# Squares of the weights queued on ScalarE behind the fourth hh eviction of their group

## The chip, the cores and the metric

The kernel runs on one core of one Trainium2 chip. The metric is the device time of one execution in microseconds, median of several. Five engines work side by side, each through its own instruction queue in order: TensorE (PE: matmuls; PEld: its weight loads), VectorE (DVE), ScalarE (ACT), GpSimd (POOL) and SyncE (SP, which here only issues DMAs). They wait for each other through semaphores.

## The reference

Three stages follow each other: a linear attention with a root-mean-square norm, then a layer of 8 experts in which each token uses its two best experts, then a second one in which each token with a positive skip score uses its best expert. All 4608 tokens have 512 numbers.

```
kv = einsum('bhsd,bhse->bhde', k, v); out = einsum('bhsd,bhde->bhse', q, kv)   # 8 x 8 x 576 x 64
x = out / rms(out) * g_norm                                                     # as 4608 rows of 512
top2 = two best of x @ w_gate + log1p(exp(x @ w_noise)) * noise                 # first expert layer
out[mask] += top2_w * (max(x[mask] @ w1[e], 0) @ w2[e])                         # w1: 512 x 1024, w2: 1024 x 512
do_compute = out @ w_skip > 0; e_idx = argmax(out @ w_gate2)                    # second expert layer
result = out + do_compute * prob * (max(out @ w21[e], 0) @ w22[e])
```

## The kernel before

Precision is made of pairs of 16-bit numbers: each matrix and each activation is held as a high half (`hi`, `hh`, `wa` or `wb` first half) and a low half (`lo`, `hl`, second half), and each product is three matmuls. Before a weight matrix can be split into halves it has to be scaled by a power of two, and the scale comes from the sum of its squares. That work is in `split_matrix` (L157 to L183):

- the load of 2 MB into a `stage` buffer (two buffers, so a third load waits until the splits of the first are done),
- four squares on ACT, L166, each over 128 x 1024, with the row sums in `wacc`,
- the sum of the four on DVE (L169, `wsum`), a matmul with ones on PE that adds over the partitions (L172),
- six small operations on DVE that make the scale `wscl` (L128 to L133, L175 to L178),
- four splits: the high half on ACT (L182), the low half on DVE (L183).

It is a generator: each `yield` hands back control, and the main loop calls `next` at set points.

The first expert layer runs in 38 groups of 256 token slots, five groups to an expert (two of the first expert's were done earlier). The fifth group of an expert has 224 slots. One group (`moe1_group`) is: layer 1, four pieces of 24 matmuls (L219) into a PSUM tile `a` (three buffers), each piece followed by `layer1_out`: ACT writes `hh` (L227), then DVE writes `hl` (L228). Then layer 2 for the two halves g0 and g1 of the group, 24 matmuls each (L255) into a PSUM tile `b` (two buffers); its first 16 matmuls read `hh` piece by piece, four matmuls to a piece, the last 8 read `hl`. ACT evicts each half as `ysb` (L1014), DVE adds the earlier expert's rows (L1018, `x`), ACT and DVE make the 16-bit halves of the result (L870, L873, L874), a DMA transposes them (L889), and one group later PE computes routing logits from them (L894, L896), DVE turns them into a choice (L899 to L934, with `rm` at L930), and PE ranks the choices (L937 to L939) between layer 2 of one group and layer 1 of the next.

`MATS` says in which group which matrix is handled: F is a matrix of the first expert layer's next expert, P one of the second layer's (`presplit`, written back to DRAM), a dot none. Per expert the pattern is F P F . P or close to it. A matrix is loaded in its group n, squared at the points 4 to 7 of group n (which lie in layer 2), and scaled and split at the points 0 to 4 of group n+1: L172 stands after the first piece of layer 1, the splits after it.

The order on PE is written out by hand (`manual_schedule`). From group `BEGIN` (3) to group `CUT + 2` (35) the order on the other engines is set by a scheduler, which takes the instructions by priority and by its own idea of when each can start; `layer1_out` and `ysb` are raised by `URGENT`. In this stretch the squares stand on ACT wherever the scheduler found ACT free.

In the groups' names below, "wa group" means the group that splits a `wa` matrix, and so on: with the pattern F P F . P the five groups of an expert are a wa group, a presplit group, a wb group, a group of 224 slots that mostly splits nothing, and a presplit group.

Of the kernel before, what the change touches and what calls it, by code (L numbers as in the profile page):

```python
# [12 lines left out]
AF = mybir.ActivationFunctionType  # L13
# [5 lines left out]
N, D, E, F = 4608, 512, 8, 1024  # L19
# [60 lines left out]
def moe_kernel(ctx: ExitStack, tc: tile.TileContext, q, k, v, g_norm, w_gate, w_noise, noise,  # L80
               w1, w2, w2_skip, w2_gate, w21, w22, out, dbg=None):
    nc = tc.nc
    V, A, G, PE, SP = nc.vector, nc.scalar, nc.gpsimd, nc.tensor, nc.sync
# [3 lines left out]
    wpools = [ctx.enter_context(tc.tile_pool(name="wpool0", bufs=1))]  # L87
    turn = {}
    stg = [None]

    def wtile(shape, dt, name, pool=None):

        turn[name] = turn.get(name, -1) + 1
        return wpools[turn[name] % len(wpools) if pool is None else pool].tile(shape, dt, name=name)
# [29 lines left out]
    def pow2_scale(ss_ps, kk, name):  # L124

        n = ss_ps.shape[-1]
        t = tiny.tile([P, n], I32, name=name + "t")
        V.tensor_scalar(t, ss_ps.bitcast(I32), 24, None, op0=ALU.logical_shift_right)  # L128
        u = tiny.tile([P, 2, n], I32, name=name + "u")
        V.tensor_scalar(u[:, 0], t, -1.0, float(kk), op0=ALU.mult, op1=ALU.add)  # L130
        V.tensor_scalar(u[:, 1], t, 1.0, float(254 - kk), op0=ALU.mult, op1=ALU.add)
        s = tiny.tile([P, 2, n], I32, name=name + "s")
        V.tensor_scalar(s, u, 23, None, op0=ALU.logical_shift_left)  # L133
        f = s.bitcast(F32)
        return f[:, 0], f[:, 1]
# [21 lines left out]
    def split_matrix(load, hi, lo, scale, kk, sc, inv):  # L157

        st = stg[0].tile([P, 4096], F32, name="stage")
        load(st)  # L160
        acc = tiny.tile([P, 4], F32, name="wacc")
        junk = tiny.tile([P, F], BF16, name="wjunk", bufs=1)
        kw = {} if scale is None else {"scale": scale}
        yield
        for c in range(4):
            A.activation(junk, st[:, F * c:F * c + F], AF.Square, accum_out=acc[:, c:c + 1], **kw)  # L166
            if c == 3:
                sums = tiny.tile([P, 1], F32, name="wsum")
                V.tensor_reduce(sums, acc, axis=AX.X, op=ALU.add)  # L169
            yield  # L170
        ps = pSm[0].tile([P, 1], F32, name="small")
        PE.matmul(ps, ones32, sums, start=True, stop=True)  # L172
        a0, i0 = pow2_scale(ps, kk, "wsc")
        if scale is None:
            V.tensor_copy(sc, a0)  # L175
        else:
            V.tensor_mul(sc, a0, scale)
        V.tensor_copy(inv, i0)  # L178
        for c in range(4):
            yield  # L180
            d = slice(F * c, F * c + F)
            A.activation(hi[:, d], st[:, d], AF.Copy, scale=sc)  # L182
            V.scalar_tensor_tensor(lo[:, d], st[:, d], sc, hi[:, d], op0=ALU.mult, op1=ALU.subtract)  # L183

    def split_half(e, wa, wb, half, hi, lo, sc, scale):
        if half == 0:
            yield from split_matrix(
                lambda st: SP.dma_start(st.rearrange("p (c f) -> p c f", f=F), wa[e].rearrange("(c p) f -> p c f", p=P)),
                hi, lo, scale, 199, sc[:, 0:1], sc[:, 1:2])
        else:  # L190
            yield from split_matrix(
                lambda st: SP.dma_start(st.rearrange("p (c d) -> p c d", d=D), wb[e].rearrange("(c p) d -> p c d", p=P)),
                hi, lo, None, 204, sc[:, 2:3], sc[:, 3:4])
# [29 lines left out]
    def layer1_out(ps, nt, hh, hl, fp):  # L223

        nf = 512 // nt
        fsl = slice(fp * nf, fp * nf + nf)
        A.activation(hh[:, fsl, 0:nt], ps, AF.Relu)  # L227
        V.scalar_tensor_tensor(hl[:, fsl, 0:nt], ps, 0.0, hh[:, fsl, 0:nt], op0=ALU.max, op1=ALU.subtract)  # L228

    def layer1_piece(W, xT, nt, hh, hl, fp):  # L230
        ps = layer1_matmuls(W, xT, nt, fp)
        with tc.high_priority(offset=URGENT):
            layer1_out(ps, nt, hh, hl, fp)
# [741 lines left out]
    def gather1(e, i0):  # L975

        t0 = e * T1 + i0
        xg = p1.tile([P, 2, XW], F32, name="xg", bufs=3)
        xT = p1.tile([P, 8, 2 * P], F16, name="xT", bufs=3)
        for g in range(2):  # L980
            G.indirect_dma_start(out=xg[:, g], out_offset=None, in_=xrows,  # L981
                                 in_offset=bass.IndirectOffsetOnAxis(ap=idx1[:, t0 + g:t0 + g + 1], axis=0))
            SP.dma_start_transpose(out=xT[:, :, g * P:g * P + P], in_=xg[:, g, 0:512].bitcast(F16))
        return xg, xT
# [64 lines left out]
    def dyn_weights(wi, pool, W, half):  # L1049
        t = wtile([P, WB], F16, "wb", pool) if half else wtile([P, WA], F16, "wa", pool)  # L1050
        G.indirect_dma_start(out=t, out_offset=None, in_=wsd[half],
                             in_offset=bass.IndirectOffsetOnAxis(ap=wi, axis=0))
        W.extend(views(t, half))
# [136 lines left out]
    def matrix(m):  # L1190
        if m is None:
            return None
        kind, e, half = m
        if half == 0:
            gens[kind] = first_weights(e, w1, w2, gcol, 0.5, Ws[e]) if kind == "first" else presplit(e)
        return gens[kind][half]
# [11 lines left out]
    for n, (e, i0) in enumerate(groups):  # L1208
        if n == BEGIN:
            begin.close()  # L1210
        if n + 1 < len(groups) and n <= BEGIN:
            xs[n + 1] = gather1(*groups[n + 1])
        if n + 2 < len(groups) and n >= BEGIN:
            xs[n + 2] = gather1(*groups[n + 2])
        if n == CUT + 2:
            order.enter_context(tc.manual_schedule(engines=engines))
        old, cur = cur, matrix(mats[n])
        if cur:
            next(cur)

        def point(p, old=old, cur=cur):
            if old and p <= 4:
                next(old, None)
                if p == 4:
                    next(old, None)
            if cur and p >= 4:
                next(cur)

        def step(k, prev=fin, last=last):
            g = last if k == 0 else prev  # L1230
            if g is not None:
                next(g, None)
            if k == 0 and n == CUT + 2:
                pick_early()
            for i in range(2):
                for what in AHEAD[i].get((n, k), ""):
                    if what == "g":
                        Ra.append(Rows(ahead[i]))
                        for _ in range(2):
                            Ra[i].gather(osc[2 * (CUT + 1 - NF0):])  # L1240
                    elif what == "s":
                        Ra[i].split()
                    else:
                        dyn_weights(ewi[:, i:i + 1], 2 * i, Wa[i], "ab".index(what))

        step(-1)
        if n == CUT + 2:
            splits.close()
            wpools.append(only1.enter_context(tc.tile_pool(name="wpool2", bufs=1)))
            p3 = only1.enter_context(tc.tile_pool(name="p3", bufs=2))  # L1250
            p4 = xrow_pool.enter_context(tc.tile_pool(name="p4", bufs=1))
            for i in range(4):
                xo.append(p4.tile([P, 1, D], F32, name=f"x2r{i}"))
                G.memset(xo[i], 0.0)
        last = fin
        fin = moe1_group(e, i0, Ws[e], *xs.pop(n), step, point)
# [18 lines left out]
    nr, nt = len(RTILES), 4 + sum(RTILES)  # L1275
# [157 lines left out]
    with flag(0):  # L1433
# [5 lines left out]
        st, cur = 1, 0  # L1439
        while st < nf:  # L1440
            V.tensor_add(inc[:, 1 - cur, st:nf], inc[:, cur, st:nf], inc[:, cur, 0:nf - st])
            V.tensor_copy(inc[:, 1 - cur, 0:st], inc[:, cur, 0:st])
            cur, st = 1 - cur, st * 2
# [134 lines left out]
```

## Time and profile before

| what | value |
|---|---|
| median of 3 runs (lowest, highest) | 1336.52 us (1332.54, 1339.37) |
| the profiled execution, its span | 1342.9 us, 1340.9 us |
| PE busy over the span | 91% |
| ACT, DVE, POOL busy over the span | 50%, 59%, 29% |
| granted TensorE clock, mean | 0.969 |
| ACT's squares L166 in all | 128, of which 96 take 1052 ns each and 32 (with `gcol`) 1143 ns |

A square with a scale from memory (`gcol`, for `w1` of the first layer) is a form of its own. Each square is followed by the read of its accumulator (185 to 200 ns, partly beside the next instruction). In a time line each row has its start, its duration, the engine, the line, the operation and how many follow each other; in brackets stands how long the engine had been idle before it and what it had waited for. The end of a matmul is modelled in the profile, so waits on PE are read better from starts than from busy time.

### The profile page before, as it was taken

What the parts mean: (1) busy time and instruction counts of PE and PEld (TensorE: products, weight loads), DVE (VectorE), ACT (ScalarE), POOL (GpSimd) and SP (SyncE); (2) the same over time, 40 slices, a digit from 0 to 9 for tenths busy, and PEclk for the clock granted to TensorE, in tenths of its full rate; (3) what the DMA queues carried; (4) which work ended last, traced back from release to release, by engine and by line L of the source; (5) the groups of instructions that cost most, each with busy time, mean ns of one, the idle gap of its engine ahead of it and who ended that gap; (6) DMA issues with size and microseconds to landing.
All of it is one profiled execution on the core that took longest, in us unless ns stands there. A gap on an engine that the chain in (4) does not pass through costs nothing.

```text
span 1340.9 us, 25198 instructions
## 1 busy us (share of the span) xinstructions
PE 1226.2 (91%) x9443; PEld 869.6 (65%) x9443; DVE 797.8 (59%) x2730; ACT 667.0 (50%) x1227; POOL 389.7 (29%) x460
## 2 busy tenths in 40 slices
PE   6777789798999999999999999999999999999996
PEld 6676676566576757666766675766575767566664
DVE  1667878134475767677668676766776765423331
ACT  2568672155565566474556666737565332222210
POOL 2322332212332323423333242342212342232220
PEclk9878889898999999999999999999999999999998
DMA  9989964758976977789598798788977494686680
GB/s 244 292 244 283 313 182 88 165 136 246 278 228 184 238 230 229 210 220 293 127 309 245 229 326 235 237 204 267 283 246 230 144 193 165 193 256 167 205 259 16
DMA packets 318751, 296.24 MB, mean 221 GB/s; under 512 B 211888, under 2 KB 263088, under 8 KB 314524
## 3 DMA queue, kind: packets, MB, share of 16 engines
q1 hardware_dynamic: 294940, 210.31, 58.3%
q0 software_dynamic: 23104, 83.18, 18.7%
q8 instruction: 76, 1.25, 0.4%
q10 hardware_dynamic: 576, 1.05, 0.2%
q14 instruction: 55, 0.45, 0.1%
HBM read 174.46 MB, written 94.73 MB: 201 GB/s over the span
## 4 chain that ended last, share of the span: by engine, by line
PE 35%; ACT 17%; issue 17%; DVE 17%; DMA 7%; POOL 4%; SPq 1%; another core or an unknown queue 0%; POOLq 0%; DVEq 0%; ACTq 0%
PE b L255 18%; PE a L219 11%; ACT wjunk L166 4%; DMA stage<-in_moe_w_dram 4%; ACT presplit L182 3%; ACT hh L227 2%; PE kvps L388 2%; ACT wa L182 2%; DVE xh L874 2%; DVE wb L183 1%; ACT wb L182 1%; DMA xg<-xrows,idx 1%; DVE hl L228 1%; POOL out_dram L1100 1%; ACT ysb L1014 1%
## 5 line engine op out<-in xcount | busy, mean ns | idle before, releaser
L219 PEld LDWEIGHTS <-wa 128*128 128x128 f16 x5184 | 473.8, 99 | 71.6 <-issue 16.3
L219 PE MATMUL a<-xT,wa 128*128 128x256 f16 (+1 forms) x3648 | 405.5, 272 | 14.4 <-DVE hl L228 12.2
L255 PE MATMUL b<-wb,hh 128*128 128x512 f16 x1536 | 352.6, 379 | 24.2 <-ACT hh L227 24.0
L255 PEld LDWEIGHTS <-hh 128*128 128x128 f16 x1536 | 143.6, 98 | 194.0 <-ACT hh L227 40.6
L227 ACT ACTIVATE hh<-a 128x512 f16<-128x512 f32 (+1 forms) x192 | 109.8, 577 | 204.1 <-PE a L219 179.5
L1021 POOL DMA_INDIRECT out_dram<-x,oi x70 | 72.9, 1042 | 422.5 <-DVE nact L949 304.3
L255 PE MATMUL b<-wb,hl 128*128 128x512 f16 x768 | 181.6, 379 | 1.1 <-DVE hl L228 1.1
L228 DVE SCALAR_TENSOR_TENSOR hl<-a,hh 128x512 f16<-128x512 f32 (+1 forms) x192 | 128.1, 674 | 86.4 <-ACT hh L227 83.8
L255 PEld LDWEIGHTS <-hl 128*128 128x128 f16 x768 | 74.9, 98 | 92.1 <-DVE hl L228 3.3
L1014 ACT ACTIVATE ysb<-b,gate 128x512 f32<-128x512 f32 x76 | 51.7, 680 | 150.4 <-PE b L255 143.8
L166 ACT ACTIVATE wjunk<-stage 128x1024 bf16<-128x1024 f32 x96 | 101.0, 1052 | 37.0 <-DMA stage<-in_moe_w_dram 23.2
L219 PE MATMUL a<-x2Tr,wa 128*128 128x256 f16 (+1 forms) x1152 | 109.2, 257 | 5.7 <-DMA x2Tr<-xh 5.3
L981 POOL DMA_INDIRECT xg<-xrows,idx x76 | 74.9, 985 | 96.3 <-DVE gate L990 57.5
L1004 POOL DMA_INDIRECT yo<-ydram,gi x70 | 79.5, 1136 | 66.9 <-issue 24.2
L183 DVE SCALAR_TENSOR_TENSOR presplit<-stage,wscl,presplit 128x1024 f16<-128x1024 f32 x64 | 80.0, 1279 | 9.5 <-ACT presplit L182 9.0
L182 ACT ACTIVATE presplit<-stage,wscl 128x1024 f16<-128x1024 f32 x64 | 70.7, 1139 | 15.2 <-DVE wscl L175 15.2
L453 PE MATMUL b<-kvbd,qTs 128*128 128x160 f32 x256 | 53.2, 348 | 20.7 <-issue 9.4
L1018 DVE TENSOR_TENSOR x<-ysb,yo 128x512 f32<-128x512 f32 x70 | 48.2, 689 | 34.7 <-ACT ysb L1014 33.7
L870 ACT ACTIVATE jk<-x 128x512 bf16<-128x512 f32 x70 | 43.9, 627 | 48.1 <-DVE x L1018 46.6
L497 POOL TENSOR_TENSOR osb<-osb,rinv 128x1024 f32<-128x1024 f32 (+1 forms) x20 | 37.3, 1863 | 87.3 <-DVE rinv L142 65.9
L453 PEld LDWEIGHTS b<-kvbd,qTs 128*128 128x128 f32 x256 | 43.5, 223 | 25.2 <-issue 11.1
L873 ACT ACTIVATE xh<-x,x2ss 128x512 f16<-128x512 f32 x70 | 47.4, 714 | 19.4 <-DVE x2ss L133 17.6
(330 smaller groups left out, 1516.0 us busy)
## 6 DMA issues: line engine op xcount, KB each, us to landing
stage<-in_moe_w_dram SPq DMA_DIRECT2D x32, 2048.0 KB
ydram<-ysb SPq DMA_DIRECT2D x66, 256.0 KB
wsd<-presplit SPq DMA_DIRECT2D x8, 2056.0 KB
wsd<-presplit SPq DMA_DIRECT2D x8, 2048.0 KB
out_dram<-zeros SPq DMA_DIRECT2D x9, 1024.0 KB
km<-in_k_dram SPq DMA_DIRECT2D x16, 512.0 KB
vm<-in_v_dram SPq DMA_DIRECT2D x16, 512.0 KB
qm<-in_q_dram SPq DMA_DIRECT2D x16, 512.0 KB
```

Of the source, the lines that this page charges most:

```text
L166: A.activation(junk, st[:, F * c:F * c + F], AF.Square, accum_out=acc[:, c:c + 1], **kw)
L182: A.activation(hi[:, d], st[:, d], AF.Copy, scale=sc)
L183: V.scalar_tensor_tensor(lo[:, d], st[:, d], sc, hi[:, d], op0=ALU.mult, op1=ALU.subtract)
L219: PE.matmul(ps[:, i, :], a[:, c, fs], xT[:, b + c, 0:nt], start=(n == 0), stop=(n == 11))
L227: A.activation(hh[:, fsl, 0:nt], ps, AF.Relu)
L228: V.scalar_tensor_tensor(hl[:, fsl, 0:nt], ps, 0.0, hh[:, fsl, 0:nt], op0=ALU.max, op1=ALU.subtract)
L255: PE.matmul(ps, a[:, f, gsl], b[:, f, :], start=(fs.start == 0 and i == 0), stop=(fs.stop == 8 and a is hl and f == 7))
L453: PE.matmul(po[:, i, :], qT[:, i, :], kvb[b % 4][:, h0 + i, :], start=True, stop=True)
L981: G.indirect_dma_start(out=xg[:, g], out_offset=None, in_=xrows, in_offset=bass.IndirectOffsetOnAxis(ap=idx1[:, t0 + g:t0 + g + 1], axis=0))
L1004: G.indirect_dma_start(out=yo, out_offset=None, in_=ydram[0:e * C1, :], in_offset=bass.IndirectOffsetOnAxis(ap=gi[:, g:g + 1], axis=0), bo ...
L1014: A.activation(ysb, ps, AF.Copy, scale=gate[:, g:g + 1])
L1021: s = G.indirect_dma_start(out=out, out_offset=bass.IndirectOffsetOnAxis(ap=oi[:, g:g + 1], axis=0), in_=x2[:, g], in_offset=None, bounds_ ...
```

## The change

The kernel keeps the latest `hh` eviction in `behind[0]`. Between group 3 and group 35 each square gets an edge to it: on ACT's queue the square stands behind that eviction. Since the squares are traced after layer 1 of their group, the eviction is the fourth one. No semaphore is added, because both run on ACT; only the scheduler's order changes.

```diff
+    behind = [None, False]
...
         for c in range(4):
-            A.activation(junk, st[:, F * c:F * c + F], AF.Square, accum_out=acc[:, c:c + 1], **kw)
+            with tc.issue_after(behind[0]) if behind[1] else ExitStack():
+                A.activation(junk, st[:, F * c:F * c + F], AF.Square, accum_out=acc[:, c:c + 1], **kw)
...
-        A.activation(hh[:, fsl, 0:nt], ps, AF.Relu)
+        behind[0] = A.activation(hh[:, fsl, 0:nt], ps, AF.Relu).ins
...
         if n == BEGIN:
             begin.close()
+            behind[1] = True
...
         if n == CUT + 2:
             splits.close()
+            behind[1] = False
```

The orders on PE and on SP are the same as before. On ACT 27 sets of four squares stand elsewhere. The lines of the changed kernel are numbered one to four higher: L168 is the square, L184 the split, L229 the `hh` eviction, L1016 `ysb`.

ACT in a wa group, before, from the last split to the next group's first `hh`: one square stands ahead of the fourth `hh`, three behind it, and the squares of the next group's matrix follow around the second `ysb`.

```order
L182 ACTIVATE wa<-stage,wscl 128x1024
L166 ACTIVATE wjunk,wacc<-stage 128x1024
L227 ACTIVATE hh<-a 128x512
L166 ACTIVATE wjunk,wacc<-stage 128x1024 x3
L1014 ACTIVATE ysb<-b,gate 128x512
L870 ACTIVATE jk,ss_4043<-x_3886 128x512
L915 ACTIVATE rdf<-rdf 128x16
L166 ACTIVATE wjunk,wacc<-stage 128x1024 x2
L1014 ACTIVATE ysb<-b,gate 128x512
L166 ACTIVATE wjunk,wacc<-stage 128x1024
L870 ACTIVATE jk,ss_4043<-x_3886 128x512
L227 ACTIVATE hh<-a 128x512
```

The same place after: the four squares stand in a row between the fourth `hh` and the first `ysb`.

```order
L184 ACTIVATE wa<-stage,wscl 128x1024
L229 ACTIVATE hh<-a 128x512
L168 ACTIVATE wjunk,wacc<-stage 128x1024 x4
L1016 ACTIVATE ysb<-b,gate 128x512
L872 ACTIVATE jk,ss_4043<-x_3886 128x512
L917 ACTIVATE rdf<-rdf 128x16
L1016 ACTIVATE ysb<-b,gate 128x512
L872 ACTIVATE jk,ss_4043<-x_3886 128x512
L229 ACTIVATE hh<-a 128x512
```

The squares that stood around the second `ysb` are gone from here; they belong to the next group and stand there behind its own fourth `hh`.

ACT from a wb group into the 224-slot group, before: squares of two matrices, the first around the fourth `hh`, the second (with `gcol`) from the first `ysb` into the next group's layer 1.

```order
L166 ACTIVATE wjunk,wacc<-stage 128x1024
L227 ACTIVATE hh<-a 128x512
L166 ACTIVATE wjunk,wacc<-stage 128x1024 x3
L1014 ACTIVATE ysb<-b,gate 128x512
L870 ACTIVATE jk,ss_4675<-x_4522 128x512
L915 ACTIVATE rdf<-rdf 128x16
L166 ACTIVATE wjunk,wacc<-stage,gcol 128x1024 x2
L1014 ACTIVATE ysb<-b,gate 128x512
L166 ACTIVATE wjunk,wacc<-stage,gcol 128x1024
L227 ACTIVATE hh<-a 128x2x224
L870 ACTIVATE jk,ss_4675<-x_4522 128x512
L166 ACTIVATE wjunk,wacc<-stage,gcol 128x1024
```

The same place after: the wb group has no squares, the 224-slot group has those of its own matrix, and the ones with `gcol` come a group later.

```order
L229 ACTIVATE hh<-a 128x512
L1016 ACTIVATE ysb<-b,gate 128x512
L872 ACTIVATE jk,ss_4675<-x_4522 128x512
L917 ACTIVATE rdf<-rdf 128x16
L1016 ACTIVATE ysb<-b,gate 128x512
L872 ACTIVATE jk,ss_4675<-x_4522 128x512
L229 ACTIVATE hh<-a 128x2x224
L875 ACTIVATE xh<-x_4522,x2ss 128x512 x2
L229 ACTIVATE hh<-a 128x2x224 x3
L168 ACTIVATE wjunk,wacc<-stage 128x1024 x4
L1016 ACTIVATE ysb<-b,gate 128x512
```

So a matrix is squared up to one group later than before, and no square is left inside layer 1.

## Rows read from the trace of the kernel before

**Rows 1.** Page, parts 1 and 2: busy us by engine; granted clock by slice.

```profile
PE 1226.2 (91%) x9443; PEld 869.6 (65%) x9443; DVE 797.8 (59%) x2730; ACT 667.0 (50%) x1227; POOL 389.7 (29%) x460
...
PEclk9878889898999999999999999999999999999998
```

**Rows 2.** Busy time by stretch, groups 3 to 34: length, engines, clock, DMA.

```profile
437.00:547.00 110.00, 107.16 (x834) 73.38 (x832) 75.64 (x288) 65.15 (x113) 35.42 (x37) 1.00 0.80 225
...
883.70:997.80 114.10, 107.91 (x838) 73.36 (x837) 80.83 (x292) 68.89 (x117) 34.22 (x36) 1.00 0.89 256
...
sum 671.00, PE 646.18 PEld 440.60 DVE 463.35 ACT 407.52 POOL 210.96; mean PE 92.31 PEld 62.94 DVE 66.19 ACT 58.22 POOL 30.14
```

**Rows 3.** Waits of PE, 345 to 1016 us: total us, times, longest.

```profile
PE b L255 <- ACT hh L227: 19.3, 25, 1.5
PE a L219 <- DVE hl L228: 3.7, 4, 1.3
PE a L219 <- issue: 0.9, 2, 0.5
PE small L894 <- DMA x2T<-xh: 0.5, 1, 0.5
```

**Rows 4.** Time line of PE: markers of groups (L172, L967, L937) and waits.

```profile
348.65 0.28 PE L172 MATMUL small<-wsum,ones 128*128 128x1 f32 x2
...
511.96 0.30 PE L967 MATMUL idx2ps<-rhs,ohp 128*128 128x160 f16 x2
...
533.28 0.30 PE L967 MATMUL idx2ps<-rhs,ohp 128*128 128x160 f16 x2
...
658.45 0.28 PE L172 MATMUL small<-wsum,ones 128*128 128x1 f32 x2
...
680.04 0.28 PE L172 MATMUL small<-wsum,ones 128*128 128x1 f32 x2
...
688.18 2.75 PE L255 MATMUL b<-wb,hh 128*128 128x512 f16 x12
691.91 1.04 PE L255 MATMUL b<-wb,hh 128*128 128x512 f16 x4 [0.97 <-ACT hh L227]
...
700.09 0.17 PE L937 MATMUL small<-rm,tri 128*128 128x16 f16 x1
...
714.82 1.04 PE L255 MATMUL b<-wb,hh 128*128 128x512 f16 x4 [0.48 <-ACT hh L227]
...
806.32 1.04 PE L255 MATMUL b<-wb,hh 128*128 128x512 f16 x4 [1.46 <-ACT hh L227]
...
997.79 0.28 PE L172 MATMUL small<-wsum,ones 128*128 128x1 f32 x2
```

**Rows 5.** Time line of ACT, the wa group of 680 us.

```profile
689.19 1.14 ACT L182 ACTIVATE wa<-stage,wscl 128x1024 f16<-128x1024 f32 x1
690.23 1.05 ACT L166 ACTIVATE wjunk<-stage 128x1024 bf16<-128x1024 f32 x1
...
691.26 0.59 ACT L227 ACTIVATE hh<-a 128x512 f16<-128x512 f32 x1
691.74 1.05 ACT L166 ACTIVATE wjunk<-stage 128x1024 bf16<-128x1024 f32 x1
...
695.15 0.67 ACT L1014 ACTIVATE ysb<-b,gate 128x512 f32<-128x512 f32 x1
```

**Rows 6.** Time line of ACT: a square that waits for its load; fourth hh.

```profile
927.94 1.06 ACT L166 ACTIVATE wjunk<-stage 128x1024 bf16<-128x1024 f32 x1 [5.50 <-DMA stage<-in_moe_w_dram]
...
940.36 0.58 ACT L227 ACTIVATE hh<-a 128x512 f16<-128x512 f32 x1
```

**Rows 7.** Time line of DVE: the same small operation twice, and L930.

```profile
680.52 0.16 DVE L131 TENSOR_SCALAR x2su<-x2st 128x2 int32<-128x2 int32 x1
...
697.46 0.17 DVE L930 TENSOR_TENSOR rm<-roh,act 128x16 f16<-128x16 f32 x1
...
1023.09 0.70 DVE L131 TENSOR_SCALAR x2su<-x2st 128x2 int32<-128x2 int32 x1
```

**Rows 8.** Time line of POOL beside the last of these.

```profile
1023.05 0.72 POOL L963 TENSOR_TENSOR rhs<-oht,vals 128x320 f16<-128x320 f16 x1 [0.23 <-DVE x2st L128]
```

## Prediction

> **What bounds the kernel now.** I read the page first: PE is busy 91% of the span and its granted clock is near full in every slice [rows 1], so time is won only where PE stands still or runs work it need not do. The change touches nothing but the order on ACT in groups 3 to 34, so I cut that stretch out with the view by stretches: over 671.0 us PE is busy 646.2, at a clock of 1.00, the upper of its two levels (2.4 GHz) [rows 2]. That leaves 24.8 us of PE idle; the clock has nothing to give back. Then the view of waits says what PE waited for there: 19.3 us in 25 waits for ACT's `hh`, 3.7 us in four for DVE's `hl`, 0.9 us without a named cause and 0.5 us for one transpose, 24.4 together [rows 3]. The reader should see that PE's losses in this stretch are nearly all of one kind and small each, at most 1.5 us.
>
> Since ends of matmuls are modelled, I also count from starts. From the marker L172 at 658.45 to that at 680.04 lies a group without any wait: 21.59 us. The 224-slot group takes 533.28 - 511.96 = 21.32 us from L967 to L967; it holds one wait, which I take like the one of 0.97 in the row at 691.91, so 20.35 without it. From 348.65 to 997.79 there are 29 groups, six of them short: 23 x 21.59 + 6 x 20.35 = 618.7 us, where the trace has 649.1 [rows 4]. By this count PE loses 30.4 us. So 24.8 and 30.4 are the two sizes of what there is to win.
>
> **The change, part by part.**
>
> *The square ahead of the fourth `hh`* (wa and wb groups, 12 in the stretch). ACT ends the last split at 690.23, then runs a square, and `hh` starts only at 691.26 [rows 5]. Meanwhile PE has started layer 2 at 688.18, has used up three pieces after 2.75 us, at 690.93, and waits 0.97 us for the fourth [rows 4]. Without the square `hh` starts 1.03 us earlier, at 690.23, and by its 0.59 us is ready at 690.82, 0.1 us before PE asks. So that wait goes, but barely: what is late next is the split ahead of `hh`. The longest wait of this sort is 1.46 us [rows 4] and keeps 0.43; four of the twelve are over 1.03, and I leave 1.3 us for them.
>
> *The squares around the second `ysb`* (presplit groups behind wa groups, six). They stand on ACT while the load is still coming: the row at 927.94 sat 5.50 us waiting for the stage [rows 6], with `ysb`, `jk` and the next group's first `hh` behind it. The splits then come in a bunch, and PE waits for the third and fourth `hh`, 0.48 us in the row at 714.82 [rows 4]; the longer `hl` waits of rows 3 are of the same groups and of the 224-slot ones. After the change these groups have the order of a wb group without its square, which by the first part just meets PE. I take 0.2 us left in each, 1.2 in all. In the 224-slot groups two that split a matrix will still be short of ACT; I estimate 0.35 us each from four splits (1.14 us a piece, rows 5) following the second `hh`, 0.7 in all.
>
> Here the trace shows something that speaks against the full gain. The operation L131 on DVE takes 0.16 us at 680.52 and 0.70 us at 1023.09, when POOL's L963 starts at 1023.05 and runs 0.72 us [rows 7, 8]. The scale for the splits now stands behind that operation in six more groups. The Trainium skill (SBUF — State Buffer, Who interferes with whom) says that VectorE and GpSimd share a pair of ports, that a VectorE operation in a two-port mode or a GpSimd one holds it for the whole instruction, and that the other blocks. The rows agree (0.54 us longer). Held to that rule in all six groups I would leave 6 x 0.54 = 3.2 us in place of 1.2, and the forecast would be 2 us higher.
>
> *The four squares ahead of the first `ysb`* (27 sets). Three squares take 695.15 - 691.74 = 3.41 us, so four take 4.55. Started at 690.23 + 0.48 (`hh` to the next start, rows 5), they end at 695.26, and `ysb` starts 0.1 us later than before, while PE is 1 us earlier. What waits behind `ysb`: DVE's sum `x`, then the choice `rm`, which PE needs for the ranking L937 between two groups. `rm` starts at 697.46 [rows 7], ends at 697.63 and would end at 697.74; L937 would come at 700.09 - 0.97 = 699.12. 1.4 us of cover are left, so I cost this at nothing. It is at most 27 sets times what exceeds the cover. The PSUM tile `b` has two buffers and is wanted again a whole half group later.
>
> *The squares a group later.* The sum is used at L172 of the next group, after the first piece of layer 1. Counted from the first `ysb` at 695.26 this is over 6 us away (in the stretch shown, L172 follows L937 by the 24 matmuls of one piece, 699.12 + 2.6). The splits do not move, so neither does the release of the stage nor the next load. A late load would now hold `ysb` and PE behind it; the load that ended at 927.94 has its squares due behind the `hh` at 940.36, 12.4 us later [rows 6]. No cost, and none of the 5.5 us waits is seen by anyone any more.
>
> *What stays.* The 0.9 us without a cause [rows 3] is no matter of ACT. Sum of what stays: 1.3 + 1.2 + 0.7 + 0.9 = 4.1 us.
>
> **Sum.** 24.8 - 4.1 = 20.7 us by the idle time, 30.4 - 4.1 = 26.3 us by the starts. Neither is better founded, so I take the middle, 23.5 us. The profiled execution took 1342.9 us, its span 1340.9 and 2.0 around it; it would become 1319.4. It is 6.4 us above the median of the runs, 1336.5; the same gain makes that 1313. What follows the stretch is bound by PE in the same way and moves forward whole.
>
> **The rivals.**
>
> *The fourth `hh` stays late.* The margin of the first part is 0.1 us. If the scale comes 0.5 us later in all 24 groups with a split (other neighbours on DVE and POOL than before), each keeps 0.4 us, 9.6 in all: gain 14, time 1322. For it: the 0.54 us of rows 7 and 8. Against: the group of 658.45 splits too and has no wait.
>
> *DMA becomes the bound.* The DMA engines are 0.80 to 0.89 busy in the stretch, and more in its later part, where an expert takes longer (110.0 and 114.1 us, rows 2). If their share cannot go over 0.90, the later experts keep their length and only the first two gain their 3.3 us each (110.0 against 4 x 21.59 + 20.35 = 106.7): 7 us, time 1330, within 0.5%. Against: DMA work of 0.89 x 114.1 = 101.5 us fits into 106.7, and PE waited 0.5 us for a transfer in the whole stretch [rows 3].
>
> *Slower: the ranking waits for the squares.* Place: L937 on PE, for DVE's `rm`, for `ysb`, for the four squares. It decides from 1.4 us of lateness on; each further us costs 27. To turn 23.5 us of gain into a loss of 7 it takes 30.5 / 27 + 1.4 = 2.5 us later in every group; the time would be 1344. Against: in the wa groups three squares stand there already, and L937 is not among PE's waits in rows 3. For: sums, choice and `x` share DVE's one queue, and the sum of the squares now stands in it ahead of the choice in 27 groups.
>
> That the change might not do what it says is excluded by the order on ACT.
>
> **How the numbers follow.** Full gain 0.70 (1313, its own range 1305 to 1320), late `hh` 0.12 (1322), DMA 0.11 (1330), ranking 0.07 (1344). The range from 1304 to 1326 holds the first two and leaves out the other two. What can be told from no change in this kernel is about 0.5%, 6.7 us: faster by more 0.82, within it 0.11, slower 0.07.
>
> **What would show each step.** In the changed profile PE's wait for `hh` in the stretch should be under 4 us in place of 19.3, for `hl` near zero; L172 to L172 should be 21.6 to 21.8 us in all full groups; the waits of `wjunk` for the stage should be gone; `ysb` should wait less for PE and stand right behind squares. A wait of PE L937 for `rm`, or waits of `wjunk` for the stage ahead of `ysb`, would prove the slower rival right; waits for `hh` of 0.3 to 0.5 us in most groups the late-`hh` one; waits of PE on `xT` or `x2T` the DMA one. If the stretch gets shorter by 20 us and the time does not, I am wrong about what follows it.

## The result, and the profile after

| | before | changed |
|---|---|---|
| median (lowest to highest), us | 1336.95 (1332.54 to 1339.37), 6 runs | 1315.94 (1315.08 to 1318.83), 6 runs |
| ratio, 95% interval | | 0.9847 (0.9827 to 0.9867) |
| profiled execution, us | 1342.9 | 1316.25 |
| its span, us | 1340.9 | 1314.3 |
| the 29 groups from the marker of [rows 4] at 348.65, us | 649.14 | 625.72 |

The change makes the kernel 21 us (1.5%) faster; 1313 was forecast. Line numbers rise by one to four: the square is L168, the split L184, `hh` L229, `ysb` L1016, the marker behind the first piece of layer 1 L174, the ranking L939, `rhs` L965. The page still has PE as the bound, with the same work [rows 1]:

```profile
PE 1225.6 (93%) x9443; PEld 871.5 (66%) x9443; DVE 793.5 (60%) x2730; ACT 674.7 (51%) x1227; POOL 387.1 (29%) x460
```

The view by stretches, for the 29 groups, first of the kernel before and then of the changed one (length; busy us of PE, PEld, DVE, ACT, POOL; clock; DMA share; GB/s):

```profile
348.65:997.79 649.14, 624.32 (x4836) 425.66 (x4834) 448.76 (x1677) 392.69 (x677) 203.89 (x212) 1.00 0.84 239
```

```profile
349.43:975.15 625.72, 621.39 (x4836) 425.81 (x4834) 445.25 (x1676) 400.19 (x677) 202.67 (x212) 1.00 0.87 249
```

The same matmuls at the same clock take 23.4 us less. PE's idle time falls from 24.8 to 4.3 us, 20.5; the other 2.9 come out of rows that count as busy (624.32 to 621.39). They are probably stalls too short to be listed; no row shows them. The profiled executions differ by 26.6 us: the stretch starts 0.8 us later in the changed kernel, and 4.0 us lie behind its end. What lies behind the end also differs by 5.9 us between two executions of the changed kernel (339.15 and, in e5 below, 345.05), so those 4.0 say nothing of the change. The execution profiled before took 6 us more than its kernel's median, so part of the 26.6 is its own; the medians say 21.

What PE waited for in the stretch (345 to 995 us), all of it, against the four lines of [rows 3]:

```profile
PE b L257 <- ACT hh L229: 4.0, 9, 0.5
```

On PE's time line, a wa group that keeps a small wait and the presplit group behind it:

```profile
671.71 0.28 PE L174 MATMUL small<-wsum,ones 128*128 128x1 f32 x2
...
682.86 1.04 PE L257 MATMUL b<-wb,hh 128*128 128x512 f16 x4 [0.25 <-ACT hh L229]
...
691.04 0.17 PE L939 MATMUL small<-rm,tri 128*128 128x16 f16 x1
...
693.74 0.28 PE L174 MATMUL small<-wsum,ones 128*128 128x1 f32 x2
...
705.35 1.04 PE L257 MATMUL b<-wb,hh 128*128 128x512 f16 x4 [0.49 <-ACT hh L229]
```

The first wait was 0.97 us in [rows 4]. The group lasts 22.03 us, 0.44 more than the 21.59 of a group without a wait. ACT in that wa group, against [rows 5]: `hh` follows the last split at once, the four squares follow it, and `ysb` follows them without idle time:

```profile
681.17 1.14 ACT L184 ACTIVATE wa<-stage,wscl 128x1024 f16<-128x1024 f32 x1
682.21 0.59 ACT L229 ACTIVATE hh<-a 128x512 f16<-128x512 f32 x1
682.69 1.06 ACT L168 ACTIVATE wjunk<-stage 128x1024 bf16<-128x1024 f32 x1
...
687.28 0.67 ACT L1016 ACTIVATE ysb<-b,gate 128x512 f32<-128x512 f32 x1
```

What is left sits in the presplit groups behind wa groups: five of the six last 22.46 to 22.49 us. Their rows on DVE and POOL show a wait that the prediction did not have:

```profile
694.85 0.14 DVE L132 TENSOR_SCALAR wscu<-wsct 128x1 int32<-128x1 int32 x1
697.33 0.17 DVE L934 COPY vals<-idv 128x4 f16<-128x4 f16 x1 [2.34 <-POOL rhs L965]
697.40 0.16 DVE L134 TENSOR_SCALAR wscs<-wscu 128x2 int32<-128x2 int32 x1
...
699.40 0.14 DVE L177 COPY wscl<-wscs 128x1 f32<-128x1 f32 x1
699.46 0.14 DVE L180 COPY wscl<-wscs 128x1 f32<-128x1 f32 x1
```

```profile
695.53 1.01 POOL L1006 DMA_INDIRECT yo<-ydram,gi  x1 [0.30 <-issue]
696.56 0.73 POOL L965 TENSOR_TENSOR rhs<-oht,vals 128x320 f16<-128x320 f16 x1
```

The copy into `vals` prepares a later group and needs a buffer that `rhs` has just read. It now stands ahead of `wscs` in the middle of the scale's chain, and `rhs` stands behind a gather. In the kernel before, the copy of such a group stood a full microsecond behind the scale, and the gather (L1004, at 707.60) behind `rhs` (706.71):

```profile
707.46 0.14 DVE L175 COPY wscl<-wscs 128x1 f32<-128x1 f32 x1
...
708.51 0.15 DVE L932 COPY vals<-idv 128x4 f16<-128x4 f16 x1
```

### The profile page after: what moved, and what is told of

It reads as the page before. It is cut to its first block, busy times and chain, and to the rows that moved or that the text cites. A ratio compares the mean times of both kernels' runs of the same rounds, so it can differ in the third digit from the quotient of the medians.

```text
span 1314.3 us, 25199 instructions
## 1 busy us (share of the span) xinstructions
PE 1225.6 (93%) x9443; PEld 871.5 (66%) x9443; DVE 793.5 (60%) x2730; ACT 674.7 (51%) x1227; POOL 387.1 (29%) x460
## 4 chain that ended last, share of the span: by engine, by line
PE 54%; DVE 12%; issue 12%; ACT 9%; DMA 7%; POOL 4%; SPq 1%; POOLq 0%; DVEq 0%; ACTq 0%
PE b L257 27%; PE a L221 21%; DMA xg<-xrows,idx 2%; ACT presplit L184 2%; DMA x2Tr<-xh 2%; PE b L455 1%; PE kvps L390 1%; DVE xh L876 1%; ACT hh L229 1%; ACT wa L184 1%; DMA x2T<-xh 1%; ACT wjunk L168 1%; DVE x L506 1%; DMA yo<-ydram,gi 1%; POOL out_dram L1102 1%
## 5 line engine op out<-in xcount | busy, mean ns | idle before, releaser
L221 PEld LDWEIGHTS <-wa 128*128 128x128 f16 x5184 | 473.9, 99 | 56.6 <-issue 11.1
L229 ACT ACTIVATE hh<-a 128x512 f16<-128x512 f32 (+1 forms) x192 | 110.6, 579 | 204.4 <-PE a L221 204.2
L1016 ACT ACTIVATE ysb<-b,gate 128x512 f32<-128x512 f32 x76 | 51.8, 681 | 122.5 <-PE b L257 122.5
L168 ACT ACTIVATE wjunk<-stage 128x1024 bf16<-128x1024 f32 x96 | 101.3, 1055 | 2.2
L184 ACT ACTIVATE presplit<-stage,wscl 128x1024 f16<-128x1024 f32 x64 | 71.2, 1140 | 35.4 <-DVE wscl L177 35.4
L171 DVE TENSOR_REDUCE wsum<-wacc 128x1 f32<-128x4 f32 x32 | 5.0, 157 | 99.5 <-ACT wjunk L168 99.5
```

The lines of the kernel that those rows point to most:

```text
L221: PE.matmul(ps[:, i, :], a[:, c, fs], xT[:, b + c, 0:nt], start=(n == 0), stop=(n == 11))
L229: behind[0] = A.activation(hh[:, fsl, 0:nt], ps, AF.Relu).ins
L1016: A.activation(ysb, ps, AF.Copy, scale=gate[:, g:g + 1])
```

## The experiments

Medians of one kernel in different rounds differ by 2 to 5 us, as much as some of the effects looked for, so each kernel is also given by the length of the 29 groups in its profiled execution, from the first to the last of the same markers. This is one execution each: the changed kernel, profiled twice, gives 625.72 and 625.75 us, the kernel of e1 and e6 gives 621.87 and 619.36. Each ratio is to the kernel before in the same rounds.

| kernel | median, us | ratio to before (95%) | 29 groups, us |
|---|---|---|---|
| before | 1336.95 | | 649.14 |
| changed | 1315.94 | 0.9847 (0.9827 to 0.9867) | 625.72 |
| e3, presplit squares queued | 1322.04 | 0.9897 (0.9860 to 0.9934) | 636.27 |
| e4, wa and wb squares queued | 1330.25 | 0.9961 (0.9932 to 0.9990) | 638.03 |
| e2, behind the third `hh` | 1326.12 | 0.9922 (0.9896 to 0.9948) | 632.87 |
| e5, changed again | 1318.22 | 0.9855 (0.9814 to 0.9897) | 625.75 |
| e1 and e6, copy for `vals` late | 1312.44, 1310.54 | 0.9846 (0.9811 to 0.9882), 0.9820 (0.9778 to 0.9862) | 621.87, 619.36 |
| e8, that alone on before | 1337.61 | 1.0006 (0.9973 to 1.0039) | 644.74 |
| e7, DVE held up | 1371.79 | 1.0252 (1.0197 to 1.0306) | 678.30 |
| e9, fifth square | 1322.23 | 0.9897 (0.9850 to 0.9945) | 634.96 |
| e10, fifth square, copy late | 1333.62 | 0.9960 (0.9934 to 0.9986) | 642.97 |
| e11, the same, `rhs` on DVE | 1308.52 | 0.9788 (0.9731 to 0.9846) | 618.73 |
| e12, changed, `rhs` on DVE | 1307.85 | 0.9774 (0.9715 to 0.9832) | 617.86 |

### The two halves of the change

e3 queues only the squares of presplit matrices, e4 only those of wa and wb (`pre` says which a matrix is; the lines that hand it through are left out):

```
-            with tc.issue_after(behind[0]) if behind[1] else ExitStack():
+            with tc.issue_after(behind[0]) if behind[1] and pre else ExitStack():      # e3
+            with tc.issue_after(behind[0]) if behind[1] and not pre else ExitStack():  # e4
```

> One part of the change alone: only the squares of matrices that go through presplit are queued behind the fourth hh. By the order on ACT this takes the square from ahead of the fourth hh in the wa and wb groups, and leaves the squares of wb around the second ysb of the presplit groups. Theory (by the waits of the trace before, 15.4 us in 14 waits at the fourth hh of wa and wb groups, of which 1.3 stay, and by the starts a little more): 14 to 17 us faster than before, 1320 to 1323 us. Rival (the hoisted squares are what delays everything behind them): under 8 us faster, 1329 us or more.

> The other part alone: only the squares of wa and wb are queued behind the fourth hh. The squares of wb no longer stand around the second ysb of the presplit groups behind wa groups; the square ahead of the fourth hh of wa and wb groups stays. Theory (by the trace before, 3.9 us of waits for hh and part of 3.7 us for hl in those groups, less about 5 us that the changed kernel still loses there): 3 to 8 us faster than before, 1329 to 1334 us; this and the other part together make the whole 21 us. Rival (the hoisted squares are the larger part): 12 us or more faster, 1325 us or less.

By the medians e3 is 14.2 us faster than before (1336.21 in its rounds) and e4 6.0, 20.1 together against 21.0 for the whole. By the 29 groups it is 12.9 and 11.1, 24.0 against 23.4. Both times are where the theory put them, though by the groups e4 gains more than the 3 to 8 us expected, and the halves add up. (e3's profiled execution, 1326.28 us, lies 4 us above its median.) In e3 the squares still sit on ACT waiting for their load, 29.1 us in six waits, and the first pieces of PE behind them wait for `hl`:

```profile
PE a L221 <- DVE hl L230: 8.2, 5, 4.0
PE b L257 <- ACT hh L229: 4.1, 12, 0.5
```

e2 puts one square back ahead of the fourth `hh`, now in every group with a split:

```
-        behind[0] = A.activation(hh[:, fsl, 0:nt], ps, AF.Relu).ins
+        r = A.activation(hh[:, fsl, 0:nt], ps, AF.Relu).ins
+        if fp == 2:
+            behind[0] = r
```

> The changed kernel with the squares queued behind the third hh of the group in place of the fourth: on ACT one square stands between the last split and the fourth hh in 24 groups, and two stand there in the 224-slot groups; nothing is hoisted a group early, and DVE, POOL, PE and SP have the orders of the changed kernel. Theory (the square ahead of the fourth hh is the price): 1.18 us from start to start of a square, less a margin of 0.1 to 0.2, in 24 groups: 24 to 28 us slower than the changed kernel, 1340 to 1344 us, so no faster than the kernel before. Rival (the hoisting was the price, the square ahead is mostly hidden): 1316 to 1326 us.

The theory missed: the stretch is 7.15 us longer than the changed kernel's, not 24 to 28, and the time sits at the rival's 1326. The square costs what I said only where the splits come late: all wa groups but the first now last 22.6 to 23.1 us. In presplit groups behind 224-slot groups the period is 21.65, so there the splits had over a microsecond to spare; and behind wa groups it is 22.35, no longer than without the square: there the copy for `vals` waited 0.59 us (at 480.74) in place of 2.34, and all its waits fell from 16.6 to 8.3 us. That the splits just meet PE was true of wa groups, not of all 24.

### What the change left

e1 queues the copy for `vals` behind the choice `rm` of its own group:

```
-        V.tensor_tensor(m16, oh, bc(act[:, :, None], s3), op=ALU.mult)
+        m = V.tensor_tensor(m16, oh, bc(act[:, :, None], s3), op=ALU.mult).ins
...
-        V.tensor_copy(vals[:, :, 0:2], idv[:, t0:t0 + 2])
+        with tc.issue_after(m) if behind[1] else ExitStack():
+            V.tensor_copy(vals[:, :, 0:2], idv[:, t0:t0 + 2])
```

> The changed kernel, and beside it the copy idv into vals on DVE (L934) is queued behind the choice rm of its own group. In the changed kernel that copy, for a later group, stands in DVE's queue ahead of the scale of the squares and waits there for POOL's rhs: 16.6 us in 11 waits. Theory (queue): this wait is what makes the fourth hh late in the nine places that are left (4.0 us); without it the periods of 22.46 us become 21.6, PE's wait for hh in the stretch falls under 1.5 us, and the time is 1310 to 1312 us, 0.980 to 0.982 of the kernel before. Rival (POOL beside DVE): DVE's small operations are slow there because POOL works at the same time (L915 took 1.95 us at 717.10); then the wait only moves into the operations behind, the fourth hh stays 0.4 to 0.5 us late in the six presplit groups, and the time stays at 1315 to 1317 us.

> The changed kernel once more, on the same chip and in the same rounds as the next three, so that they can be compared with it. Expected from its earlier runs: 1314 to 1319 us, 0.983 to 0.987 of the kernel before; nine waits for hh in the stretch, the six of 0.49 us in presplit groups behind wa groups among them.

> The kernel of e1_late_vals once more, beside the changed kernel on one chip. Its six times lay from 1308.7 to 1320.2 us, too wide to tell 4 us. Theory (the wait of the copy for vals, 5.3 us by the periods of six groups): 3 to 6 us under the changed kernel's median of the same rounds. Rival (the profiled run was a lucky one, the waits for hh cost nothing by the end): within 2 us of it.

> The kernel before, with the copy idv into vals queued behind rm of its own group and nothing else. There the copy waited 4.2 us in 7 waits, and in presplit groups behind wa groups it stands behind the scale of the squares, not ahead of it. Theory (the wait ahead of the scale is made by the change): within 3 us of the kernel before. Rival (the copy delays the fourth hh in both kernels): 4 us or more faster than the kernel before.

ACT, POOL, PE and SP keep their orders. In e1 the presplit groups behind wa groups last 21.59 us; its median, 1312.44, is just above the 1310 to 1312 expected, with a wait of 2.0 us for a transpose in its stretch. PE's waits in the 29 groups of e6 are down to these:

```profile
PE b L257 <- ACT hh L229: 0.3, 1, 0.3
PE small L896 <- DMA x2T<-xh: 0.3, 1, 0.3
```

e5 came at 1318.22 us, as expected, with ten waits for `hh` in place of nine. In the same rounds e6 has a median 7.7 us under e5's, more than the 3 to 6 expected, though the single times overlap (1307.4 to 1318.1 against 1313.5 to 1323.3); the 29 groups are 6.4 us shorter.

On the kernel before, the same edit shows nothing by the median (1337.61 against 1337.05 in the same rounds), but its interval (0.9973 to 1.0039) reaches from 3.6 us faster to 5.2 slower, and its 29 groups are 4.4 us shorter. The periods say where. The presplit groups behind wa groups do not gain (22.75 to 24.10 us in e8, 22.66 to 24.06 before): there the wait is one that the change made, by the place that it gave the copy. Of the six wa groups four last 22.03 us in e8 where they lasted 22.55 to 23.11. In these the copy stood ahead of `wscs` in the kernel before too, and in three of the four it waited 0.6 us for `rhs`:

```profile
461.36 0.17 DVE L932 COPY vals<-idv 128x4 f16<-128x4 f16 x1 [0.61 <-POOL rhs L963]
461.43 0.16 DVE L133 TENSOR_SCALAR wscs<-wscu 128x2 int32<-128x2 int32 x1
...
463.50 0.15 DVE L178 COPY wscl<-wscs 128x1 f32<-128x1 f32 x1
```

PE's wait in that group, before and in e8:

```profile
470.42 1.04 PE L255 MATMUL b<-wb,hh 128*128 128x512 f16 x4 [1.19 <-ACT hh L227]
```

```profile
472.43 1.04 PE L256 MATMUL b<-wb,hh 128*128 128x512 f16 x4 [0.26 <-ACT hh L228]
```

So the rival of e8 holds in the wa groups and the theory in the others. Not all of the gain in the wa groups is the copy's own wait, because the chain of the scale also starts 0.7 us earlier there in e8; but a wa group of e4 whose chain starts as early (at 457.44), with the copy ahead of `wscs`, still lasts 23.13 us.

How the square and the late scale add up can be read from the periods. The scale's time is that of its last row (the copy into `wscl` at L178, L179 or L180), counted from the marker of its group:

| group (its marker) | square ahead of the fourth `hh` | scale, us behind the marker | period, us |
|---|---|---|---|
| e8, wa (461.28) | yes | 4.24 | 22.03 |
| before, wa (680.04) | yes | 4.94 | 22.74 |
| before, wa (458.34) | yes | 5.16 | 22.96 |
| changed, wa (455.95) | no | 4.99 | 21.75 |
| changed, wa (671.71) | no | 5.26 | 22.03 |
| changed, presplit behind wa (693.74) | no | 5.72 | 22.49 |

In these rows the period is 21.59 us plus what the scale comes later than 3.80 us with the square, and later than 4.83 us without it, to 0.01 us. The square is worth the 1.03 us of the prediction, and each microsecond that the scale is late costs the same as a microsecond of squares. Groups that lose time in another way do not follow this, such as the first wa group of the kernel before (22.40 us with the scale at 3.27).

The rival of e1, DVE slowed by POOL's work, falls as the cause of the losses in presplit groups: its longest row is the same in e1 and in the changed kernel, and stands in a wb group ahead of a 224-slot group, which lasts 21.38 us in both with no wait of PE. It is not quite free there: in e12, without `rhs` on POOL, the group lasts 21.27.

```profile
708.50 1.95 DVE L915 TENSOR_SCALAR rsc<-x2ss,rsk 128x2 f32<-128x2 f32 x1
```

### The slower rival: the ranking waits for the squares

e7 holds DVE up between the squares and the choice:

```
+                if behind[1]:
+                    V.tensor_reduce(sums, acc[:, 3:4].to_broadcast([P, 3072]), axis=AX.X, op=ALU.add)
                 V.tensor_reduce(sums, acc, axis=AX.X, op=ALU.add)
```

> The changed kernel, and on DVE ahead of each of the 27 sums of squares a reduction over 3072 columns, some 3.2 us, whose result is overwritten. It stands behind the squares and ahead of x and of the choice rm. This tries the slower rival at its own place: in the changed kernel rm ends 1.3 to 2.0 us before PE's ranking L939, 2.9 us where ysb does not stand behind squares. Theory (the ranking holds PE up as soon as the cover is used): rm comes about 3.2 us later, PE waits 1.2 to 1.9 us for it in about 20 groups, 25 to 45 us slower than the changed kernel, 1341 to 1361 us. Rival (the ranking has slack that the row does not show): within 5 us of the changed kernel.

```profile
PE small L941 <- DVE rm L934: 35.0, 20, 2.4
PE b L259 <- ACT hh L231: 11.5, 18, 1.0
```

The rival's mechanism exists: the reduction takes 3.35 us, and that turns the gain into a loss of 34.7 us against before; it is 53.6 against the changed kernel of the same rounds, where 25 to 45 were expected. 35.0 of it are the ranking, as expected (20 waits); the expectation missed the scale, which is late as well (11.5 us of waits for `hh`).

e9 asks the same of ACT, with a fifth square ahead of `ysb`; e10 adds the late copy, e11 moves `rhs` to DVE as well:

```
+        more4 = tiny.tile([P, 4], F32, name="wmore")
...
+                for x in range(1 if c == 3 and behind[1] else 0):                                      # e9
+                    A.activation(junk, st[:, 0:F], AF.Square, accum_out=more4[:, x:x + 1])
```
```
-        G.tensor_tensor(rhs, bc(oht[:, :, None, :], [P, 2, 4, NS2]), ...
+        (V if behind[1] else G).tensor_tensor(rhs, bc(oht[:, :, None, :], [P, 2, 4, NS2]), ...        # e11, e12
```

> The changed kernel with a fifth square (a repetition whose sum is not used) behind the four of each set: it stands ahead of the first ysb of the group in 26 of 27 places, 1.18 us from start to start. Theory (the squares ahead of ysb are covered as far as the choice rm ends 1.3 to 2.9 us before the ranking L939): the fifth still fits, and the stretch from the first L174 marker over 29 groups grows by at most 3 us from 625.7 us; time within 4 us of the changed kernel, 1312 to 1322 us. Rival (the four squares use up the cover already, the ranking waits for each further one): 20 to 27 sets at 1 us, 20 to 30 us slower, 1336 us or more, with PE's waits for rm in the trace.

> e9_fifth_square with the copy for vals queued behind rm, as in e1_late_vals; the fifth square stays ahead of the first ysb. In e9 the stretch of 29 groups took 634.96 us, 9.2 us over the changed kernel, without any wait of PE for rm: its waits were for hh, 10.1 us in 16, and DVE's waits of vals for rhs had grown from 16.6 to 26.5 us. Theory (the squares ahead of ysb cost nothing by themselves; what e9 lost came through the copy that waits ahead of the scale): the stretch takes 619 to 622 us, as in e1 and e6, and PE's waits for hh are under 2 us; time 1308 to 1316 us. Rival (five squares make everything behind ysb late, so the scale and the fourth hh too): the stretch stays over 628 us, with over 5 us of waits for hh.

> The kernel of e10_fifth_and_late, and rhs is worked out on DVE in place of POOL in the groups of the stretch. In e10 the theory failed: the stretch took 642.97 us, and a new kind of wait stood there, DVE's wsct 39.3 us in 16 and ACT's first hh 52.4 us in 15 for a signal of PE whose matmul had started up to 5 us earlier; nearly each of these waits ended within 0.5 us of the end of POOL's rhs, which follows two to four gathers and scatters. Theory (what holds the signals is POOL's run of gathers that ends with rhs): without rhs on POOL these waits end about 1 us earlier, at the end of the last gather, and the stretch shrinks by 5 to 15 us, to 628 to 638 us. Rival A (rhs itself holds them): the waits vanish, the stretch takes 619 to 624 us. Rival B (the signal is late on PE's side, POOL's end is a coincidence): waits as in e10, stretch over 638 us.

In e9 PE never waits for `rm`, so the cover ahead of the ranking holds for 1.18 us more; the least that is left of it is 0.34 us. But the stretch grows by 9.2 us, three times what the theory allowed, and its waits are for `hh`, with 26.5 us of the copy for `vals` waiting. The scheduler also changed the order on DVE and POOL in e9, so it is no trial of ACT alone. e10, which should have taken the copy's wait away, is worse: 642.97 us. The rival's numbers are met (over 628 us, 7.5 us of waits for `hh`), its mechanism is not what the trace shows. A kind of wait stands in it that the changed kernel does not have, and whose releaser the trace doesn't name ("remote"). ACT's first `hh`, DVE's `wsct` and a weight load of PE that stood without a named cause all go on at 483.65 to 483.74 us, though the matmul that `wsct` needs started at 478.63:

```profile
483.69 0.60 ACT L232 ACTIVATE hh<-a 128x512 f16<-128x512 f32 x1 [5.39 <-remote]
```

```profile
483.74 0.16 DVE L129 TENSOR_SCALAR wsct<-small 128x1 int32<-128x1 int32 x1 [4.25 <-remote]
```

```profile
482.64 0.73 POOL L969 TENSOR_TENSOR rhs<-oht,vals 128x320 f16<-128x320 f16 x1
```

All sixteen of DVE's waits of this kind end within 0.02 us of the end of `rhs` or up to 0.5 us behind it. So do the two that the kernel before has (at 682.32 and 796.74). With `rhs` on DVE (e11) they are gone, as its rival A had it, and the stretch takes 618.73 us with all five squares in it, 0.9 more than e12 below without the fifth. So the fifth square is nearly free, and the e10 loss needs `rhs` on POOL. That is not enough for it, because the changed kernel has `rhs` on POOL and no such wait. Why a signal of PE should come late beside it stays open: the edit also takes POOL's run of work apart, and no run here separates the two.

### The best version

> The changed kernel with rhs worked out on DVE in place of POOL in the groups of the stretch: the copy for vals then has nothing on POOL to wait for, and stands where it stood. On ACT three splits in place of two follow the second hh in some groups. Theory (the wait of vals for POOL is the 5 us that the change left): the period of the presplit groups behind wa groups falls from 22.46 us to 21.6 to 21.9, and the stretch takes 619 to 623 us. Rival (one more DVE operation ahead of the scale and the later first split cost as much as the wait did): 624 to 630 us.

e12 is the changed kernel with `rhs` on DVE (0.49 us each there, 0.73 on POOL). PE waits for nothing in its 29 groups, which take 617.86 us, under the 619 to 623 expected, where the prediction counted 618.7 without any wait. At 1307.85 us it has the lowest median of all, 0.9774 of before, though its interval overlaps the changed kernel's and they did not run in the same rounds.

## Why the prediction was right, point by point

**What bounds the kernel.** Right. The winnable part was sized twice, 24.8 us by idle time and 30.4 by starts. Idle time gave 20.5 (forecast 20.7). The starts gave 23.4 (forecast 26.3). The floor behind the second count, 618.7 us, is met by e12, so counting from starts is the better founded of the two. That the middle, 23.5, came out at 23.4 is luck: its base (the mean of 24.8 and 30.4) is 2.8 us under the count by starts, and the 4.1 taken off it for what stays are 2.9 too little. By the medians the gain is 21, 2.5 under the forecast.

**The square ahead of the fourth `hh`.** Right: the waits of the wa and wb groups went, e3 alone, which takes the square from there, is worth 14.2 us, and the table above gives the square the 1.03 us forecast. Left by the periods over 21.59 are 2.2 us in the wa groups (one alone has 0.9) and 0.3 in one wb group, where 1.3 was forecast. Most of it is the scale held by the copy for `vals`, not the split: in e6 all wa groups but one last 21.60 us or less. (The longest wait of this sort before is 1.49 us, at 964.25, not 1.46; nothing hangs on it.)

**The squares around the second `ysb`.** Right that they cost PE (e4); mis-sized in what stays: 0.2 us in each of six groups was forecast, 1.2 in all, and five groups kept 0.87 to 0.90, 4.5. The failed step is "these groups have the order of a wb group without its square, which by the first part just meets PE". That was read from ACT's order alone. On DVE the copy for `vals` had moved ahead of the scale, and on POOL a gather ahead of `rhs`; neither was costed, and together they held the scale 2.34 us; e1 and e6, which take the copy from there, have these groups at 21.59 to 21.60. The 0.7 us for 224-slot groups and the 0.9 without a cause did not appear. Together 7.0 us stayed, not 4.1.

**DVE beside POOL.** What stood in these groups was a wait for a buffer. The longest rows of DVE stand elsewhere and cost about 0.1 us there: L915 takes 1.95 us at 717.10 in the changed kernel, while a gather and `rhs` run on POOL from 716.75 to 718.53, in a group of 21.38 us (21.27 in e12). By the rule of the Trainium skill (SBUF — State Buffer, Who interferes with whom) I would have left 3.2 us in these groups, which lies nearer to the 4.5 measured than my 1.2, but for another reason. The trace agrees with the rule itself in that row, and does not show it at 694.65, where the same operation takes 0.23 us while a scatter runs on POOL from 694.21 to 695.23.

**Squares ahead of `ysb`, and a group later.** Right: no wait of the ranking in the stretch; the waits of the squares for the stage are gone from ACT's list. The cover, 1.4 us in the prediction, is 1.28 us in the group shown above (`rm` ends at 689.76, L939 starts at 691.04) and takes a fifth square (e11).

**The rivals.** *Late fourth `hh`*: true in nine places of 24, for 4.0 us, and by this rival's own mechanism, a scale that comes late because of its neighbours on DVE and POOL. *DMA the bound*: refuted; its share rose to 0.87, in e12 to 0.90 and in e11 to 0.91 over the whole stretch, and the full groups without a wait stayed at 21.59. *The ranking*: a real mechanism that the change does not reach (e7).

## What to carry to other kernels

When an instruction is queued elsewhere, read the order of every engine around it, not only of its own: a harmless copy that the scheduler puts into the gap can carry a wait into the middle of a critical chain. An instruction whose only dependence is a buffer to come free should be tied behind work that is surely later than that release. And where PE is the bound, count a stretch from start to start between markers: it shows stalls that the busy rows hide, and leaves out what differs elsewhere (625.72 and 625.75 us for two executions of the changed kernel that differ by 7.0 in all). One execution still has stalls of its own, so compare it group by group.

## What the runs showed of the hardware

The two profiled executions of the changed kernel (1316.25 us and, in e5, 1323.25) differ by 1.1 us ahead of the stretch, by 0.03 in it and by 5.9 behind it. Within the stretch the granted clock was 1.00 in both. Ahead of it, in the first 100 us, the mean was 0.81 in both and 0.88 in e6 (of the two levels, 1.2 and 2.4 GHz, a mixture); the first marker came at 349.43 and 350.50 us against 345.39. The kernel before had 0.88 there as well and its first marker came at 348.65, so the clock of those 100 us does not set that time by itself.

ACT and DVE went on up to 5 us after the start of the matmul whose result they read, in sixteen groups of one kernel (e10) and in two of the kernel before, with no releaser that the trace names. No other run here has a wait of this kind in the stretch. All these waits of DVE ended within 0.5 us of the end of `rhs` on POOL, and they were gone when `rhs` left POOL (e11); the cause is open.

An operation of DVE on 128x2 numbers (L915) took 1.95 us at 717.10 in the changed kernel, while a gather and `rhs` ran on POOL, and 0.23 us at 694.65 beside a scatter.
